# The first nine chunks of a recurrent layer, written as one list of 472 steps

## The chip, the core and the metric

The kernel runs on one core of a Trainium2 chip. Its engines are TensorE (PE, with its weight loads as PEld), VectorE (DVE), ScalarE (ACT), GpSimd (POOL) and SyncE (SP), which here issues nearly all DMAs. The metric is the device time of one execution in microseconds.

## What is computed

A recurrence over 768 time steps for 4 x 8 heads with a 40 x 40 state, and behind it two layers on the 3072 x 320 result, in float32:

```python
for t in range(S):
    y[:, :, t] = np.einsum('bhd,bhde->bhe', rt, state)
    Sa = np.einsum('bhde,bhe->bhd', state, at)
    state = state * wt[:, :, None, :] - np.einsum('bhd,bhe->bhde', Sa, bt)
    state = state + np.einsum('bhd,bhe->bhde', vt, kt)
...
h = np.maximum(np.maximum(x @ w1, x @ w2), x @ w3); x = h @ w_out              # Moe1, 768 wide
h = x @ w_in; g = h * np.tanh(softplus(h)); out = g @ w_out                    # Moe2, 2048 wide
```

## The kernel before

**Chunks, units, solves.** The recurrence is cut into chunks of 32 steps, two groups of 24, so 48 chunks. A *unit* is the preparation of two chunks (24 units, `pre`): a scan of the decays w on DVE (L253), logarithm and exponential on ScalarE for the inverse (L264, L266), two corrections on DVE (L276, L278), a square on ScalarE (L280), two scalings of the keys on DVE (L285, L287), four multiplications of ax on POOL (L272), 64 small matmuls into a PSUM bank, a copy to `ab` (ScalarE, L307), a transpose (DVE, L311) and four masks on POOL (L318). A *solve* takes the `ab` of four units: one transpose, then 31 pairs of a product and a subtraction, each on the result of the last (L346, L348), then a transpose back (L352). Solves 0 and 1 run on DVE, later ones on POOL. `kb` (L363, L367) transposes a unit's keys into `ls`.

**A chunk** (`chain`) has five stages, each on the result of the last: x0 (PE) and its copy X0 (ScalarE, L427); u; uT; the products on PE and rs on DVE (L461); ys on PE (L474), then the next state sv (L479) and YT (L481) on DVE. Chunk c needs its unit, the solve of the unit's four and sv of chunk c-1. Every second chunk's YT goes out by DMA to `xs`, from where Moe1 loads it.

**Weight tiles.** Moe1's weights come as 24 tiles of 64-bit numbers (18 of w1, w2, w3 and 6 of w_out). `from64` loads one into a staging buffer `raw`, of which there are four as of `t`; then one step on ScalarE and two on DVE (L672, L675, L676), one addition on POOL (L678), casts on ScalarE (L687) and two subtractions on POOL (L693, L732).

**Order.** `start` writes out units 0 to 3, solve 0 and the conversions beside it. `run` then goes through chunks and five slots of each: in a slot one stage of the chunk, `fill`, steps of the next units (`advance`), steps of the solve, and `kb`. Up to chunk 4 (`LAG`) `fill` takes one step of the pipelined conversions a slot; at chunk 4 it ends them and opens Moe1, whose groups of 256 tokens then take four chunks each: 18 products of seven matmuls, then 48 matmuls in steps of eight. Up to chunk 9 (`HAND`) all five engines issue in the order in which the program is written; behind it PE, DVE and ScalarE do, and the compiler orders POOL and SP. Each engine works strictly in its order, so what waits holds all that is queued behind it. Moe1's groups run on to the end of the chunks, then Moe2 follows.

Of the kernel before, what the change touches and what calls it, by code (L numbers as in the profile page):

```python
# [8 lines left out]
F32 = mybir.dt.float32  # L9
# [86 lines left out]
FREE = 0  # L96
CONV = 6
# [3 lines left out]
MID = 6  # L101
STEPS = (1, 1, 1, 1, 1)
HOLD = (7, 0)
CATCH = 8
# [59 lines left out]
class Attention:  # L164
# [56 lines left out]

    def load_w(self, n):
# [22 lines left out]
    def pre(self, n):  # L245
# [62 lines left out]
        if n < NB:  # L308
            yield
# [86 lines left out]
    def chain(self, c):  # L396
# [36 lines left out]
        yield  # L433
# [10 lines left out]
        yield  # L444
# [12 lines left out]
        yield  # L457
# [8 lines left out]
        yield  # L466
# [35 lines left out]
    def start(self, convert):  # L502
        nc, A = self.nc, self.A
        self.under, self.next, self.done, self.held, self.solved, self.turn = [], 0, 0, False, 0, 0
# [8 lines left out]
        nc.vector.memset(self.ax[0], 0.0)  # L513
        nc.vector.memset(self.zero, 0.0)
        nc.vector.memset(self.rst, 0.0)
        nc.vector.memset(self.rst[:, 0:528:C + 1], 1.0)
        for n in range(NB):
            if n:
                nc.gpsimd.memset(self.ax[n], 0.0)
            self.load_w(n)  # L520
            self.load_a(n)
            self.load_k(n)
        for t in self.sv:
            nc.gpsimd.memset(t, 0.0)
        nc.scalar.copy(out=self.ys.rearrange("p w x -> p (w x)")[:, 0:512], in_=self.rst[:, 0:512])
        nc.scalar.copy(out=self.ys.rearrange("p w x -> p (w x)")[:, 512:528], in_=self.rst[:, 512:528])
        for t in self.rs:
            zeros(t[32:64])
        for _ in range(3):
            convert()  # L530
        nc.sync.dma_start(out=self.cst, in_=A["cst"])
        for t in self.rs:
            nc.sync.dma_start(out=t[0:40, 4:9], in_=A["rsi"])
        self.load_v(0)
        self.load_chunk(0)
        nc.vector.memset(self.ls[0], 0.0)
        units = [self.pre(n) for n in range(NB)]
        self.next = NB

        def go(n, steps):  # L540
            for _ in range(steps):
                next(units[n], None)

        go(0, 2)
        nc.vector.memset(self.ls[1], 0.0)
        go(1, 2)
        go(0, 6)
        go(2, 2)
        go(1, 5)
        go(0, 2)  # L550
        go(1, 1)
        go(3, 2)
        go(2, 5)
        go(1, 2)
        go(2, 1)
        go(3, 5)
        go(2, 2)
        convert()
        go(3, 1)
        solve = self.solve(0)  # L560
        next(solve)
        go(3, 3)
        self.done = NB
# [822 lines left out]
```

## Time and profile before

| | |
|---|---|
| median of three runs | 1040.8 us (1040.03 to 1041.81) |
| the profiled execution | 1039.32 us, its span 1037.6 us |
| busy: PE, DVE, ACT, POOL | 914.8, 749.4, 735.7, 483.6 us |
| granted TensorE clock, mean | 0.958 of full speed |

The page's 40 slices of 25.9 us show PE at 4, 0, 3, 5, 6, 8, 7 tenths and then at 8 and 9; DVE begins at 8, 9, 7, 5, 6, 7, 8 tenths, POOL at 8, 4, 6, 8. The slices show that the first fifth of the time is another regime than the rest; they don't show which engine limits it, for which the stages have to be looked at one by one.

### The profile page before, as it was taken

The numbers are of one execution on the slowest core, as the hardware profiler recorded it, in microseconds if no ns is written. First come the engines' busy times: TensorE is split into PE (matmuls) and PEld (weight loads), VectorE is DVE, ScalarE is ACT, GpSimd is POOL, SyncE is SP. The second block draws the span as 40 slices with busy tenths as digits, with TensorE's granted clock in tenths as the row PEclk, the third lists the DMA queues.
The fourth block names the chain that finished last, engine by engine and source line by source line (L and its number), as shares of the span: only waits on it lengthen the run. The fifth ranks groups of instructions, "written<-read, shape, count | busy, mean of one in ns | idle before, by whom it ended". The sixth has DMA issues, their size and how long they took to land.

```text
span 1037.6 us, 34156 instructions
## 1 busy us (share of the span) xinstructions
PE 914.8 (88%) x14098; PEld 823.1 (79%) x14098; DVE 749.4 (72%) x1411; ACT 735.7 (71%) x1858; POOL 483.6 (47%) x715
## 2 busy tenths in 40 slices
PE   4035687899999999999999999979999999999996
PEld 3024576788889888898988988968898899889885
DVE  8975678566675556566366667698998888898875
ACT  5357644466777567577678977878797988878874
POOL 8468513569969947974943434780202011020000
PEclk9998586899999999999999999999999999999999
DMA  8638422345454444445356454420100010010000
GB/s 235 178 97 213 121 57 61 86 116 140 122 138 107 136 130 118 116 110 146 87 139 163 116 148 144 119 74 1 57 1 31 26 32 26 15 42 1 26 1 29
DMA packets 117334, 96.07 MB, mean 93 GB/s; under 512 B 73316, under 2 KB 93412, under 8 KB 117172
## 3 DMA queue, kind: packets, MB, share of 16 engines
q1 hardware_dynamic: 116432, 93.59, 33.4%
q8 instruction: 113, 1.85, 0.8%
q14 instruction: 49, 0.40, 0.1%
q10 hardware_dynamic: 740, 0.23, 0.1%
HBM read 81.20 MB, written 12.58 MB: 90 GB/s over the span
## 4 chain that ended last, share of the span: by engine, by line
PE 59%; DVE 14%; POOL 14%; ACT 6%; issue 5%; DMA 3%; SPq 0%; ACTq 0%; DVEq 0%; POOLq 0%
PE cops L1092 5%; PE cops L1093 5%; PE cops L1094 5%; PE ys L474 5%; PE cps L742 4%; PE cps L743 4%; PE cps L744 4%; PE bps L742 4%; PE bps L915 4%; POOL T L348 3%; POOL tv L346 3%; POOL ax L272 3%; PE bps L743 3%; PE bps L744 3%; PE cps L746 2%
## 5 line engine op out<-in xcount | busy, mean ns | idle before, releaser
L742 PE MATMUL bps<-bxh,bw 128*128 128x256 f32 x432 | 140.4, 326 | 4.6 <-DVE mx L874 3.4
L743 PE MATMUL bps<-bxl,bw 128*128 128x256 f32 x432 | 124.5, 288 | 3.3 <-DVE bxl L755 3.3
L744 PE MATMUL bps<-bxh,bw 128*128 128x256 f32 x432 | 123.2, 285 | 0.0
L1045 POOL CAST cxh<-cxl 128x512 fp32r<-128x512 f32 x15 | 12.0, 835 | 187.8 <-DMA cxl<-x 187.8
L742 PEld LDWEIGHTS bps<-bxh,bw 128*128 128x128 f32 x432 | 83.0, 192 | 13.7 <-DVE mx L874 3.8
L743 PEld LDWEIGHTS bps<-bxl,bw 128*128 128x128 f32 x432 | 83.8, 194 | 5.4 <-DVE bxl L755 5.4
L479 DVE TENSOR_TENSOR sv<-ys,pp 40x320 f32<-40x320 f32 x92 | 44.9, 488 | 55.6 <-PE ys L474 54.9
L744 PEld LDWEIGHTS bps<-bxh,bw 128*128 128x128 f32 x432 | 83.7, 194 | 0.0
L272 POOL TENSOR_TENSOR ax<-ax,pp 40x256 f32<-40x256 f32 x96 | 72.6, 774 | 20.9 <-DVE pp L253 9.3
L877 POOL TENSOR_TENSOR hl<-mx,hh 128x256 fp32r<-128x256 f32 x72 | 55.5, 771 | 56.0 <-ACT hh L876 54.8
L461 DVE TENSOR_TENSOR rs<-cgps,cst 64x256 f32<-64x256 f32 x96 | 40.6, 423 | 56.6 <-PE cgps L391 54.5
L1088 DVE TENSOR_TENSOR gl<-e,gh 128x512 fp32r<-128x512 f32 x93 | 69.9, 752 | 14.4 <-ACT gh L1087 13.4
L348 POOL TENSOR_TENSOR T<-T,tv 128x31 f32<-128x31 f32 (+15 forms) x124 | 74.7, 603 | 8.6
L318 POOL TENSOR_SCALAR_AFFINE_SELECT ax<-akT 32x256 f32<-32x256 f32 x96 | 49.0, 510 | 63.5 <-DVE akT L311 58.9
L915 PE MATMUL bps<-hh,bo 128*128 128x256 f32 x360 | 77.3, 297 | 0.6 <-ACT mx L872 0.6
L1076 ACT ACTIVATE e<-e 128x512 f32<-128x512 f32 x93 | 58.6, 630 | 24.9 <-DVE e L1074 24.4
L1080 DVE SCALAR_TENSOR_TENSOR e<-e,r 128x512 f32<-128x512 f32 x93 | 68.6, 737 | 8.7 <-ACT r L1078 8.6
L874 DVE TENSOR_TENSOR mx<-bps,mx 128x256 f32<-128x256 f32 x144 | 60.2, 418 | 19.4 <-ACT mx L872 11.7
L474 PE MATMUL ys<-rs,ls 128*40 128x72 f32 x1536 | 66.6, 247 | 7.9 <-DVE rs L461 5.7
L346 POOL TENSOR_TENSOR tv<-tr,T 128x31 f32<-128x31 f32 (+15 forms) x124 | 68.3, 551 | 11.2 <-DVE tr L339 3.0
L474 PEld LDWEIGHTS ys<-rs,ls 128*40 128x40 f32 x1536 | 57.8, 130 | 14.6 <-issue 5.8
L1073 ACT ACTIVATE e<-cps 128x512 f32<-128x512 f32 x93 | 54.7, 588 | 18.9 <-PE cps L746 18.8
(243 smaller groups left out, 3153.1 us busy)
## 6 DMA issues: line engine op xcount, KB each, us to landing
bk<-in_KB_dram SPq DMA_DIRECT2D x24, 448.0 KB
sv<-in_SV_dram SPq DMA_DIRECT2D x96, 80.0 KB
raw<-in_w_dram SPq DMA_DIRECT2D x18, 384.0 KB
again<-in_w_dram SPq DMA_DIRECT2D x27, 256.0 KB
w<-in_W_dram SPq DMA_DIRECT2D x21, 231.0 KB
v<-in_VT_dram SPq DMA_DIRECT2D x48, 96.0 KB
rs<-in_RT_dram SPq DMA_DIRECT2D x48, 96.0 KB
cxl<-x SPq DMA_DIRECT2D x12, 384.0 KB
```

The source lines that it names most:

```text
L272: nc.gpsimd.tensor_tensor(out=xv[:, h], in0=xv[:, h], in1=P[ro, h, 0:C], op=ALU.mult)
L346: eng.tensor_tensor(out=tv, in0=abT[:, s, s + 1:C].unsqueeze(2).to_broadcast([128, n, s + 1]), in1=T[:, s, 0:s + 1].unsqueeze(1).to_broadc ...
L348: eng.tensor_tensor(out=T[:, s + 1:C, 0:s + 1], in0=T[:, s + 1:C, 0:s + 1], in1=tv, op=ALU.subtract)
L474: nc.tensor.matmul(out=self.ys[64 * y:64 * y + 40, p, 0:72], lhsT=l[:, y, p], rhs=r_[:, :, 4 * (p % 4) + 2 * (1 - y) + p // 4], start=True ...
L742: nc.tensor.matmul(out=ps, lhsT=h[:, k], rhs=xh[:, k], start=(k == 0), stop=False)
L743: nc.tensor.matmul(out=ps, lhsT=h[:, k], rhs=xl[:, k], start=False, stop=False)
L744: nc.tensor.matmul(out=ps, lhsT=l[:, k], rhs=xh[:, k], start=False, stop=False)
L874: after(1, lambda ps=ps, mx=mx: nc.vector.tensor_tensor(out=mx, in0=ps, in1=mx, op=ALU.max))
L915: nc.tensor.matmul(out=pss[d][rows], lhsT=lhsT, rhs=rhs, start=first, stop=last)
L1076: nc.scalar.activation(out=e, in_=e, func=AF.Square, bias=1.0)
L1080: nc.vector.scalar_tensor_tensor(out=e, in0=e, scalar=1.0, in1=r, op0=ALU.add, op1=ALU.mult)
L1088: nc.vector.tensor_tensor(out=gl, in0=e, in1=gh.bitcast(F32), op=ALU.subtract)
```

## The change

`start` no longer ends with solve 0. It reads a list, `START`, of 472 entries, each a letter and a number, and does one step for each; the list goes to the end of chunk 8, and `run` begins at chunk 9. The letters: u a step of unit n, x its four multiplications of ax on POOL (now a step of their own, `mult`), c a stage of chunk n, e a step of solve n, w a step of weight tile n, f `fill` of a slot (chunk times five and slot), k half a `kb`; W, A, K, V, L the loads of a unit's w, a, keys, of a chunk's v and of a chunk; m, s, l, R, z, Z, U clears; p the constants of the scan, C, D loads of constants, r the first products.

Besides: a chunk's stage pauses once, not twice, and a slot takes one step of it; units 0 to 3 pause where later ones do; a tile pauses once behind its load, not three times; the two PSUM banks of Moe1 come from two pools of one in turn; each unit's bank for the inverse is named in `BANKS`, as it was before; `kb` of a unit waits until its keys are scaled.

The core of the diff (the removed body of `start`, which the words above tell, and the other four stages of the chunk, edited alike, are left out):

```diff
 NPOOL = 14
 NE = 3
-FREE = 0
-CONV = 6
 HAND = 9
 PACE = 2
 UD = 8
-MID = 6
-STEPS = (1, 1, 1, 1, 1)
+BEGIN = 9
+BANKS = 'ucucppxxssssssss'
+START = """
+m0 m1 K0 W0 W1 A0 W2 m2 A2 A1 K1 W3 K2 m3 A3 s1 V0 K3 w0 w1 w2 l1 s0 C l0 p R1 R0 u0 u0 u1 x0 u1 x1 u0 u0 u0
+u0 u2 u2 u0 u0 u0 u1 u1 x2 u0 u0 u1 u1 L0 u1 u1 u1 u3 x3 u3 u2 u2 u2 u2 u2 u2 u1 u1 u2 u3 u3 u3 l2 u3 u3 w3 u2
+w0 u2 u3 w0 u3 w1 w4 z5 A5 e0 L1 w1 u3 z6 A6 D w2 u3 e0 e0 e0 w5 z4 e0 e0 w1 e0 e0 w3 w0 r V1 e0 z7 A7 A4 e0
+w3 e0 w2 e0 e0 w0 e0 e0 w6 e0 e0 K4 K5 U w3 e0 e0 w1 e0 w4 e0 e0 e0 e0 w5 e0 e0 w6 w7 k0 w3 w5 w2 w2 k1 w5 w4
+w4 w4 w6 w8 w5 e0 e0 e0 e0 e0 e0 e0 e0 Z0 c0 w7 K6 w7 w6 c0 u4 w8 u4 c0 w9 w6 w10 w8 Z1 x4 w11 w12 w9 c0 w7 u4
+u4 w8 V2 c0 w11 w9 w13 u4 u5 w7 L2 w9 c1 A8 w8 w9 w10 w11 w10 k2 w14 w12 w10 u4 u5 x5 c1 w15 u5 w10 w11 u4 u4
+w12 w16 c1 w13 w11 w12 w14 c1 w13 w17 w14 u4 w18 u4 w15 w13 c1 u5 w12 k3 V3 w14 u5 K7 w13 w15 w19 w14 u4 w16
+u5 L3 w17 w17 u5 c2 w15 w16 w20 c2 u5 w18 c2 w15 w18 w19 u5 w17 w21 u5 c2 V4 c2 w18 k4 w17 u5 w19 w19 w20 c3
+w18 w22 w23 w20 L4 w20 K8 w21 c3 w23 w19 w20 c3 w21 w23 w22 k5 w21 c3 w22 w23 w23 A9 u6 w21 V5 w16 c3 w16 L5
+x6 w22 w22 c4 f20 u6 u6 c4 f21 u6 c4 u6 u6 u7 u7 c4 u7 V6 x7 f22 u6 u7 c4 K9 u7 u6 u6 u6 u6 L6 c5 f23 u7 u7 u7
+f24 f25 u7 e1 c5 f26 A10 u7 e1 e1 e1 e1 e1 c5 f27 c5 V7 f28 u7 e1 e1 e1 e1 c5 f29 k6 k7 e1 c6 c6 f30 c6 e1 e1
+L7 e1 e1 e1 f31 e1 e1 e1 c6 V8 e1 e1 e1 c6 k8 e1 f32 f33 e1 u8 u8 e1 L8 e1 e1 x8 c7 A11 e1 f34 u8 f35 e1 e1 u8
+c7 f36 u8 u8 e1 e1 c7 u8 u8 e1 u9 x9 u8 u9 f37 u8 e1 c7 u9 f38 u8 u9 c7 f39 V9 k9 L9 u9 K10 u9 u10 u10 u9 x10
+c8 f40 u10 u10 c8 f41 u9 u9 u9 c8 f42 u10 u11 x11 u9 c8 f43 K11 u10 c8 f44 u10 V10 u11 u11 L10
+"""
 HOLD = (7, 0)
+LAST = 8
...
+    def mult(self, n):
+
+        if n in self.multiplied:
+            return
+        self.multiplied.add(n)
+        x, P = self.ax[n % self.NX], self.pp[n % self.NP][0:R]
+        for y in range(2):
+            ro = slice(64 * y, 64 * y + 40)
+            xv = x[ro, y].rearrange("r p c t -> r (p c) t")
+
+            for h in (slice(0, 8), slice(8, 16)):
+                self.nc.gpsimd.tensor_tensor(out=xv[:, h], in0=xv[:, h], in1=P[ro, h, 0:C], op=ALU.mult)
...
         nc.scalar.activation(out=Q, in_=Q, func=AF.Exp, scale=-1.0, accum_out=self.gate.le(1e5, R))
-        for y in range(2):
-            ro = slice(64 * y, 64 * y + 40)
-            xv = x[ro, y].rearrange("r p c t -> r (p c) t")
-
-            for h in (slice(0, 8), slice(8, 16)):
-                nc.gpsimd.tensor_tensor(out=xv[:, h], in0=xv[:, h], in1=P[ro, h, 0:C], op=ALU.mult)
+        if not self.written:
+            self.mult(n)
         yield
 
         t = w.rearrange("r (q t) -> r q t", q=16)[0:R, :, 1:33]
...
         nc.vector.tensor_tensor(out=bv[:, 8:16], in0=bv[:, 8:16], in1=Qv[:, 8:16], op=ALU.mult)
-        if n >= NB:
-            yield
+        yield
+        self.scaled = n + 1
+        self.mult(n)
         while n >= NB and (self.turn < n or self.solved < self.batch[n]):
             yield
         if n < NB:
-            ps = self.ps_st.tile([128, 2, 4, 64], F32, name="m1", tag="b")
+            ps = self.ps_st[n % 2].tile([128, 2, 4, 64], F32, name="m1", tag="b")
         else:
             ps = self.ps_un.tile([128, 2, 4, 64], F32, name="m1", tag="un")
-        self.held = n >= NB
+            self.held = True
...
         nc.scalar.copy(out=self.ab[:, i:i + 8], in_=psv[:, :, C:2 * C])
-        if n < NB:
-            yield
+        yield
         akT = p1.tile([128, 4, 2, C], F32, name="akT")
...
         st_out(0)
         yield
-        yield
 
...
+        units, self.chains, self.solves = {}, {}, {}
+        steps = {}
+        def clean(n):
+            (nc.vector if n == 0 else nc.gpsimd).memset(self.ax[n], 0.0)
+        def unit(n):
+            if n not in units:
+                units[n] = self.pre(n)
+                steps[n] = 0
+            steps[n] += 1
+            if next(units[n], "end") == "end":
+                assert n == self.done, n
+                self.done += 1
+                del units[n]
+        def chain(c):
+            if c not in self.chains:
+                self.chains[c] = self.chain(c)
+            next(self.chains[c], None)
+        def substitute(k):
+            if k not in self.solves:
+                self.solves[k] = self.solve(k)
+            next(self.solves[k], None)
+        def constants():
+            nc.sync.dma_start(out=self.cst, in_=A["cst"])
+        def pattern():
+            nc.vector.memset(self.zero, 0.0)
+            nc.vector.memset(self.rst, 0.0)
+            nc.vector.memset(self.rst[:, 0:528:C + 1], 1.0)
+            nc.scalar.copy(out=self.ys.rearrange("p w x -> p (w x)")[:, 0:512], in_=self.rst[:, 0:512])
+            nc.scalar.copy(out=self.ys.rearrange("p w x -> p (w x)")[:, 512:528], in_=self.rst[:, 512:528])
+        def rows():
+            for t in self.rs:
+                nc.sync.dma_start(out=t[0:40, 4:9], in_=A["rsi"])
+        does = dict(u=unit, x=self.mult, c=chain, e=substitute, w=lambda t: next(tiles[t], None),
+                    f=lambda x: fill(x // 5, x % 5), p=lambda _: pattern(), C=lambda _: constants(), D=lambda _: rows(),
+                    Z=lambda i: zeros(self.ys[32:64, 4 * i:4 * i + 4]), z=lambda n: zeros(self.ax[n]), m=clean,
+                    s=lambda i: nc.gpsimd.memset(self.sv[i], 0.0), R=lambda i: zeros(self.rs[i][32:64]),
+                    l=lambda i: nc.vector.memset(self.ls[i], 0.0), U=lambda _: zeros(self.ud), W=self.load_w, A=self.load_a,
+                    K=self.load_k, V=self.load_v, L=self.load_chunk, k=lambda x: self.kb(x // 2, x % 2),
+                    r=lambda _: self.products(None, 0))
+        for x in START.split():
+            x, _, n = x.partition("*")
+            for _ in range(int(n or 1)):
+                does[x[0]](int(x[1:] or 0))
+        self.written = False
+        self.next = max(steps) + 1
+        self.under = [[units[n], steps[n]] for n in sorted(units)]
...
-        k, left = 0, 0
+        k = max(self.solves, default=-1)
+        solve = self.solves.get(k, iter(()))
+        left, due = (40, 2 * (self.last[k - 1] + 1)) if k in self.solves else (0, 0)
         halves = []
-        for c in range(NC):
+        for c in range(BEGIN, NC):
             n, cc = divmod(c, 2)
-            chain = self.chain(c)
+            chain = self.chains.get(c) or self.chain(c)
             if c == HAND:
...
-                if (c, slot) == (0, 4):
-                    for u in range(self.NK, AHEAD):
-                        self.load_k(u)
-                for _ in range(0 if c < FREE else PACE if LAG <= c < 2 * NB else 1):
-                    self.advance(min(NT, MID if c < LAG else AHEAD if (c, slot) < HOLD else 12 if c < CATCH else m + (cc == 1 and slot > 0)))
+                for _ in range(PACE if LAG <= c < LAST else 1):
+                    self.advance(min(NT, AHEAD if (c, slot) < HOLD else 12 if c < CATCH else m + (cc == 1 and slot > 0)))
...
-                next(chain, None)
                 if cc == 1 and slot in (0, 2) and n + 1 < NT:
                     halves.append((n + 1, slot // 2))
-                while halves and not self.held:
+                while halves and not self.held and halves[0][0] < self.scaled:
                     u, g = halves.pop(0)
...
-    for _ in range(3 if later else 2):
+    for _ in range(1 if later else 2):
...
-        self.ps = pool("b_ps", 2, space=PSUM)
+        self.ps = [pool(f"b_ps{i}", 1, space=PSUM) for i in range(2)]
-        self.banks = 2 * [self.ps]
+        self.banks = list(self.ps)
...
-                weights = pipelined(moe1.weights(), 1)
+                tiles = list(moe1.weights())
-                    for _ in range(STEPS[slot]):
-                        convert()
                     q, r = divmod(c - LAG, 4)
                     if q == 0 and (r, slot) == (0, 0):
-                        finish(weights)
+                        for t in tiles:
+                            finish(t)
                         moe1.open()
                     if (c, slot) == (2 * NB, 0):
                         moe1.third()
```

## Rows read from the trace of the kernel before

**Rows 1.** Windows: busy us by engine, instructions, clock, DMA share; cuts: chunk starts (L427).
```profile
core 0: us, PE busy (x) PEld busy (x) DVE busy (x) ACT busy (x) POOL busy (x), PEclk, DMA share, GB/s
0.00:24.70 24.70, 9.76 (x287) 8.31 (x288) 19.90 (x32) 13.77 (x31) 20.71 (x38) 1.00 0.90 233
24.70:58.30 33.60, 2.86 (x47) 2.00 (x43) 31.00 (x79) 11.50 (x26) 13.46 (x21) 1.00 0.59 159
...
60.80:74.50 13.70, 7.10 (x174) 5.72 (x174) 9.03 (x17) 9.56 (x29) 12.76 (x19) 1.00 0.39 120
74.50:92.30 17.80, 8.25 (x234) 6.69 (x235) 10.16 (x20) 12.52 (x38) 16.64 (x25) 1.00 0.83 224
92.30:105.90 13.60, 7.87 (x238) 6.38 (x240) 8.53 (x18) 8.67 (x27) 11.76 (x19) 0.58 0.66 181
105.90:116.60 10.70, 7.57 (x182) 6.33 (x184) 5.20 (x11) 7.79 (x23) 7.52 (x14) 0.50 0.33 86
116.60:129.10 12.50, 8.20 (x238) 6.86 (x239) 8.79 (x14) 7.82 (x24) 5.25 (x8) 0.50 0.59 135
129.10:147.40 18.30, 16.15 (x294) 14.25 (x294) 13.05 (x32) 6.72 (x20) 4.24 (x9) 0.73 0.21 51
147.40:164.80 17.40, 12.81 (x226) 11.40 (x226) 16.37 (x41) 5.14 (x17) 1.47 (x2) 0.80 0.24 54
164.80:189.70 24.90, 18.96 (x338) 16.46 (x334) 19.48 (x39) 13.50 (x37) 12.89 (x17) 0.73 0.27 75
189.70:205.80 16.10, 12.93 (x274) 11.59 (x274) 9.54 (x16) 6.71 (x22) 9.80 (x13) 0.79 0.33 86
205.80:638.00 432.20, 420.12 (x9434) 382.35 (x9431) 259.86 (x538) 311.17 (x972) 286.51 (x453) 0.99 0.48 125
```

**Rows 2.** Windows, as above: chunks 10 to 13, four of the later ones.
```profile
220.30:265.40 45.10, 43.83 (x1024) 39.92 (x1023) 28.06 (x54) 31.34 (x97) 39.49 (x64) 1.00 0.46 123
```

**Rows 3.** Windows, as above: stages A, B and C of the ramp.
```profile
0.00:60.80 60.80, 12.63 (x328) 10.31 (x328) 53.27 (x114) 27.61 (x60) 35.32 (x61) 1.00 0.69 183
60.80:116.60 55.80, 30.79 (x820) 25.12 (x822) 32.93 (x64) 38.55 (x114) 48.67 (x74) 0.80 0.59 161
116.60:205.80 89.20, 69.04 (x1354) 60.56 (x1353) 67.22 (x139) 39.89 (x116) 33.65 (x48) 0.72 0.31 76
```

**Rows 4.** POOL, 0 to 205.8: line op out<-in xcount | busy, mean ns | idle, releasers.
```profile
L272 POOL TENSOR_TENSOR ax<-ax,pp 40x256 f32<-40x256 f32 x48 | 33.8, 723 | 16.6 <-PE bps L746 7.0 <-DVE pp L253 5.9 <-PE kb L363 2.5
L678 POOL TENSOR_TENSOR t<-t,raw 128x384 int32<-128x384 int32 (+1 forms) x24 | 24.2, 1011 | 14.3 <-DVE t L676 13.1
...
L693 POOL TENSOR_TENSOR bw<-t,bw 128x256 fp32r<-128x256 f32 x18 | 13.1, 728 | 1.2 <-ACT bw L687 1.0
L732 POOL TENSOR_TENSOR bw<-t,bw 64x128 fp32r<-64x128 f32 x18 | 8.2, 454 | 1.4
```

**Rows 5.** The same view of ScalarE, 24.7 to 58.3.
```profile
L511 ACT COPY ax<-zero 128x1024 f32<-128x1024 f32 x4 | 3.9, 1038 | 0.0
```

**Rows 6.** Waits of DVE and of SP's queue, 0 to 206: total us, times, longest.
```profile
DVE t L676 <- POOL bw L732: 5.0, 4, 2.1
...
SPq L661 <- POOL t L678: 39.1, 13, 6.2
```

**Rows 7.** DVE by line, 0 to 205.8, columns as in rows 4.
```profile
L348 DVE TENSOR_TENSOR T<-T,tv 128x31 f32<-128x31 f32 (+15 forms) x62 | 21.0, 339 | 2.1
L676 DVE SCALAR_TENSOR_TENSOR t<-raw,bits 128x384 int32<-128x384 int32 (+1 forms) x24 | 12.9, 538 | 7.2 <-POOL bw L732 5.0
L675 DVE TENSOR_SCALAR bits<-raw 128x384 int32<-128x384 int32 (+1 forms) x24 | 12.9, 536 | 4.1 <-DMA raw<-in_wo_dram 2.5 <-DMA raw<-in_w_dram 1.4
L346 DVE TENSOR_TENSOR tv<-tr,T 128x31 f32<-128x31 f32 (+15 forms) x31 | 12.3, 396 | 0.8
```

**Rows 8.** Timeline of POOL and DVE at 143.7: start us, us, engine, line, operation.
```profile
143.75 0.73 POOL L877 TENSOR_TENSOR hl<-mx,hh 128x256 fp32r<-128x256 f32 x1 [4.92 <-ACT hh L876]
...
143.78 0.91 DVE L346 TENSOR_TENSOR tv<-tr,T 128x175 f32<-128x175 f32 x1
145.09 0.37 DVE L346 TENSOR_TENSOR tv<-tr,T 128x192 f32<-128x192 f32 x1
```

More of the change, by code (lines that the diff above doesn't have):

```diff
@@ L255, in pre @@
         yield
-        if NB <= n < 2 * NB:
-            Q = (self.ps_st if n < MID else self.extra).tile([128, 16, C], F32, name="Qx", tag="b")[0:R]
-        elif n >= NB:
+        where = BANKS[n] if n < len(BANKS) else "s"
+        if where == "s":
             Q = p1.tile([128, 16, C], F32, name="Q", tag="Q")[0:R]
-        elif n % 2:
+        elif where == "c":
             Q = self.cg[0:R].rearrange("p (q t) -> p q t", q=16)
+        elif where == "u":
+            Q = self.ps_un.tile([128, 16, C], F32, name="Qp", tag="un")[0:R]
         else:
-            Q = self.ps_un.tile([128, 16, C], F32, name="Qp", tag="un")[0:R]
+            Q = (self.ps_st[n % 2] if where == "p" else self.extra).tile([128, 16, C], F32, name="Qx", tag="b")[0:R]
         nc.scalar.activation(out=Q, in_=Pv, func=AF.Ln)
         nc.scalar.activation(out=Q, in_=Q, func=AF.Exp, scale=-1.0, accum_out=self.gate.le(1e5, R))
-        for y in range(2):
-            ro = slice(64 * y, 64 * y + 40)
-            xv = x[ro, y].rearrange("r p c t -> r (p c) t")
-            for h in (slice(0, 8), slice(8, 16)):
-                nc.gpsimd.tensor_tensor(out=xv[:, h], in0=xv[:, h], in1=P[ro, h, 0:C], op=ALU.mult)
+        if not self.written:
+            self.mult(n)
         yield
@@ L443, in chain @@
         st_out(1)
-        yield
         yield
@@ L500, in advance, with start @@
                 self.done += 1
-    def start(self, convert):
+    def start(self, tiles, fill):
         nc, A = self.nc, self.A
-        self.under, self.next, self.done, self.held, self.solved, self.turn = [], 0, 0, False, 0, 0
+        self.under, self.done, self.held, self.solved, self.turn = [], 0, False, 0, 0
+        self.written, self.multiplied, self.scaled = True, set(), 0
         def zeros(*ts):
@@ L511, in zeros @@
                 nc.scalar.copy(out=t, in_=z.to_broadcast(list(t.shape)))
[L513 to L529, printed above, removed]
-            convert()
[L531 to L563, printed above, removed]
-        self.turn = NB
-        convert()
-        nc.vector.memset(self.ls[2], 0.0)
-        zeros(self.ud)
-        self.products(None, 0)
-        self.load_v(1)
-        self.load_chunk(1)
-        for n in range(NB, AHEAD):
-            zeros(self.ax[n])
-            self.load_a(n)
-            if n < self.NK:
-                self.load_k(n)
-        for s in range(C - 1):
-            next(solve)
-            if s % CONV == CONV - 1:
-                convert()
@@ L580, in start @@
-        for g in range(2):
-            self.kb(0, g)
-        finish(solve)
-        for g in range(2):
-            zeros(self.ys[32:64, 4 * g:4 * g + 4])
+        units, self.chains, self.solves = {}, {}, {}
[11 more added lines that the diff above has]
+                del units[n]
@@ L586, in run @@
+        for x in START.split():
[5 more added lines that the diff above has]
+        self.under = [[units[n], steps[n]] for n in sorted(units)]
     def run(self, fill):
         NT, NC = 2 * NU, 2 * NCH
-        solve = iter(())
-        k, left = 0, 0
+        k = max(self.solves, default=-1)
+        solve = self.solves.get(k, iter(()))
+        left, due = (40, 2 * (self.last[k - 1] + 1)) if k in self.solves else (0, 0)
@@ L1332, in program @@
                 with tc.manual_schedule(engines=IN_ORDER | {mybir.EngineType.Activation, mybir.EngineType.Pool, mybir.EngineType.SP}):
-                    att.start(convert)
+                    att.start(tiles, fill)
                     next(chunks)
```

5 lines of the change are left out of this document (removed).

## The prediction

> **What bounds the kernel now.** I first read the busy time of each engine by stage, cut at the start of each chunk's first copy (X0, line 427). Behind chunk 9 the kernel is bound by TensorE: 420.1 of 432.2 us busy at a granted clock of 0.99, and four chunks with a whole Moe1 group take 45.1 us with 43.8 of them on PE [rows 1, 2]. So a chunk with its quarter of a group costs about 11 us there, and nothing of that part is edited. The list ends where chunk 9 begins, at 205.8 us. So the question is how early chunk 9 can begin; from there on each microsecond is kept, as long as the same work has been done by then.
>
> By then it has. The list issues fills 20 to 44, all 24 weight tiles, chunks 0 to 8, solves 0 and 1, transposes up to unit 4 and loads up to unit 11 and chunk 10; units 10 and 11 stand in the middle, as in the old trace. It is a permutation: DVE still has its 153.4 us, POOL its 117.7, ACT its 106.1 [rows 3]. The floor for chunk 9 is therefore about 158 us (DVE's sum and the 4.8 us that it is idle in the first 24.7, [rows 1]), and the most that can be won is 205.8 - 158 = 48 us.
>
> Then I asked stage by stage which engine is full. **A, 0 to 60.8**: DVE, 53.3 of 60.8 us [rows 3]. **B, chunks 0 to 3**: POOL, 48.7 of 55.8; DVE has only 32.9 [rows 3]. It converts weight tiles without a break, at 1.01 + 0.73 + 0.45 = 2.2 us for a tile [rows 4], and the chunks take 13.7, 17.8, 13.6 and 10.7 us where 11 would do [rows 1]. **C, chunks 4 to 8**: nobody for the whole stretch. DVE has 67.2 of 89.2 [rows 3]; it is nearly full in chunk 6 (16.4 of 17.4) and idle three to four tenths of the time in chunks 4, 5 and 8; the clock stands at 0.50 to 0.80 [rows 1].
>
> **The change, stage by stage.** *A.* The first solve keeps its place: the chain of 31 products and subtractions on DVE, 33.6 us with 31.0 busy, and five conversions go beside it in the list as in the trace [rows 1]. Ahead of it, unit 1's scan now runs while unit 0 waits for ScalarE, and the first two W loads come sooner; against it the load K0 is issued ahead of W0. DVE is busy 19.9 of the first 24.7 us [rows 1], so at most 4.8 us are there. I take -1, bounds -3 and +3. The clears of units 4 to 7 and the loads between the solve's steps are hidden: ACT is busy 11.5 of 33.6 us and the DMA engines 0.59 of it [rows 1]. Without that cover the four clears would cost 4 x 1.04 us [rows 5].
>
> *B.* The sum is made on POOL, since DVE's share is smaller. The list leaves some 17.6 of 24 tiles for this stage, and I count 49 us of POOL work from chunk 0's first step to chunk 4's, of which the last 2.7 (unit 6's four multiplications, 4 x 0.72 less overlap [rows 4]) need not be done when chunk 4 starts. So POOL alone allows 46 us. It is uneven: 8, 20, 7 and 14 us from chunk 0 on. What the chunks then take is the larger of that and their own 11: about 12, 16, 11 and 11, 50 us in place of 55.8. I take -6; bounds -10 (POOL's 46 exactly) and +2 (the waits of the next sentence). DVE's second conversion step waits for a staging buffer that POOL gives back, 5.0 us in four such waits [rows 6]; the same chunks' rs, sv and YT are queued on DVE behind it, and PE behind those. With two, three or four tiles in flight all through the list this wait stays; I leave it at its old size.
>
> *C.* The list puts the second solve's 34 steps between chunk 5's first step and chunk 7's fourth, in effect where they were, but with the other units between. Counting the list at the durations of the trace (a product 0.40 and a subtraction 0.34 in the mean [rows 7], the rest likewise), DVE gets 9, 15, 19, 17 and 7 us in chunks 4 to 8, 67 in all, as in the old trace [rows 3]. Where DVE has less than 11 the chunk's own chain decides, 11 to 12 us; where it has more, DVE does: 11.5 + 16 + 19 + 17 + 11.5 = 75 us in place of 89.2. I take -14. Bounds: -20 (chunk 8 and chunk 4 at 10.7, no gap on DVE) and 0 (the gaps of 5 to 7 us on DVE in chunks 5, 7 and 8 come back, at a low clock). PE is no second bound at full clock (11 us a chunk, [rows 2]); at half clock a chunk would want up to 22, and chunk 5 shows it: 16.2 of 18.3 us on PE at 0.73 [rows 1]. [...]
>
> One thing speaks against filling DVE and POOL side by side. While POOL ran a subtraction of 0.73 us, a product of the second solve took 0.91 us; the next, longer one took 0.37 [rows 8]. That is 0.5 us for a collision. The list puts two units' multiplications and two masks beside this solve, perhaps ten POOL instructions more than stood there; 0 to 5 us, and I take 1, within the 75. The Trainium skill, "SBUF — State Buffer", section "SBUF: two separate sides", says that a VectorE instruction with two SBUF inputs and a GpSimd one that reads SBUF exclude each other for the whole instruction; the row agrees in direction, and by the rule each collision would hold the loser for the rest of the other instruction, 0.7 us at most, some 5 to 7 us where I take 1.
>
> *Small edits, taken at nothing.* The multiplications of ax as a step of their own (x): the same four POOL instructions. One yield in a chunk's stage and one call in a slot: the same order behind chunk 9. Two one-bank pools in place of one of two banks, used in turn: the same rotation. One pause in place of three behind a tile's load matters only through the list. SP's queue gets W, A, K, V, chunk and weight loads in the list's order; in the old trace it waited 39.1 us in all for POOL to give staging back [rows 6], which cost only where a tile was then late. Bounds -2 and +4, in stage B.
>
> **Sum.** -1 - 6 - 14 = -21. Chunk 9 starts near 185 in place of 205.8 us. The profiled execution took 1039.3 us (1037.6 of span and 1.7 around it), 1.5 under the median of 1040.8; so 1018.3 against it and 1020 against the median.
>
> **The rivals.**
> *DVE filled almost whole.* If the interleaving leaves DVE hardly a gap, chunk 9 starts near 170: 36 us won, 1005. For it: DVE ran without a gap through chunk 6 already [rows 1]. Against it: DVE's work in chunks 2, 3, 4 and 8 is under 9 us each in the list, less than a chunk's chain.
> *Stage B moves, C doesn't.* If PE stays at half clock in chunks 5 to 7, they keep 18, 17 and 20 us or so, and C gives 5 at most: -1 - 3 - 3 = -7, 1034. For it: clock 0.73 to 0.80 in all three [rows 1]. Against: DVE, not PE, is the fuller engine in chunk 6.
> *The list does nothing to the end.* It would have to be that the Moe1 groups, not the chunks, set the time behind chunk 9 and are as late as before: 1040. Against it: the first group's fills are written at fixed places among the chunks.
> *Slower.* All five engines follow the written order through the ramp, and it is a new one, and four staging buffers are shared by 24 tiles. Tile 16's last two steps stand behind chunk 3's third stage, 50 and more entries after its third step; if a later tile's step on DVE or SP has to wait for that buffer, DVE stands still with the chunk behind it. Each such wait costs most of a chunk, some 10.7 us [rows 1]; one leaves a gain of 10, from the second on the change is lost, three give 1040.8 - 21 + 32 = 1052. Against it: the old waits of this kind were 2.1 us at most [rows 6].
>
> **How the numbers follow.** Forecast (gain 10 to 30) 0.63; DVE nearly full 0.12; B alone 0.13; nothing 0.04; slower 0.08. A measurement can tell about 0.2%, 2 us, from no change. The second rival's lower end falls within that by 0.01, and of "nothing" 0.01 falls past it, so faster is 0.63 + 0.12 + 0.12 = 0.87, same 0.04, slower 0.09. The range leaves out 2 in 10: it runs from 1005 (the first rival; the forecast's ends, -3 - 10 - 20, give 1007) to 1035 (just past the second rival), and leaves out the outer half of the first rival, a quarter of the second, and the last two.
>
> **What would show it.** Right in A: the first chunk's X0 copy at 57 to 62 us. In B: X0 of chunk 4 at 107 to 113, and POOL over 90% busy between. In C: chunks 5 to 7 at 15 to 19 us with DVE over 90% busy, chunks 4 and 8 under 13. X0 of chunk 9 at 180 to 190, and from it to the end 832 us as before. Wrong: DVE waits for POOL or a DMA of over 5 us in one piece, clock at 0.50 through chunk 6, or a stretch behind chunk 9 that is longer than 832 because POOL and SP, which are ordered anew there, fall otherwise.

## The result, and the profile after

The changed kernel takes 1033.06 us (median of five runs, 1030.22 to 1034.91), the kernel before beside it 1040.8 (1039.09 to 1042.47); the ratio of the two is on record as 0.9905, with a 95% interval of 0.9884 to 0.9926. So 8 us are won by the medians, 8 to 12 by the interval, where 21 were forecast. The direction and the range hold, the size doesn't.

The windows of the changed kernel, cut as [rows 1] at the start of each chunk's first copy (X0, now line 452), same columns; the first row is stage A, the next four B, the next five C, then chunk 9:

```profile
core 0: us, PE busy (x) PEld busy (x) DVE busy (x) ACT busy (x) POOL busy (x), PEclk, DMA share, GB/s
0.00:59.50 59.50, 12.62 (x328) 10.30 (x328) 52.57 (x113) 27.36 (x60) 37.90 (x64) 1.00 0.74 197
59.50:69.70 10.20, 5.58 (x165) 4.57 (x166) 6.74 (x13) 8.90 (x27) 9.29 (x15) 1.00 0.42 111
69.70:90.00 20.30, 11.47 (x276) 9.14 (x278) 16.16 (x31) 13.67 (x39) 18.89 (x28) 1.00 0.62 173
90.00:102.30 12.30, 8.53 (x214) 6.78 (x214) 5.07 (x12) 7.95 (x24) 8.51 (x14) 1.00 0.64 160
102.30:111.70 9.40, 5.90 (x168) 5.04 (x170) 6.34 (x12) 7.82 (x23) 8.08 (x12) 0.63 0.61 167
111.70:122.50 10.80, 8.17 (x240) 6.66 (x241) 7.73 (x13) 7.82 (x23) 7.48 (x13) 0.53 0.64 156
122.50:140.20 17.70, 15.34 (x298) 13.57 (x296) 14.75 (x36) 6.87 (x21) 5.13 (x9) 0.81 0.19 40
140.20:157.60 17.40, 11.40 (x214) 10.32 (x214) 16.27 (x41) 6.83 (x21) 2.17 (x3) 0.80 0.35 80
157.60:177.40 19.80, 16.41 (x332) 14.57 (x333) 17.30 (x36) 11.68 (x33) 11.33 (x18) 0.89 0.14 36
177.40:188.90 11.50, 11.31 (x277) 9.96 (x276) 9.07 (x15) 6.71 (x21) 7.68 (x11) 0.89 0.74 194
188.90:207.50 18.60, 15.46 (x328) 13.58 (x325) 10.72 (x21) 9.80 (x29) 6.23 (x10) 0.82 0.50 134
```

Against [rows 1, 3] the stages stand so (profiled executions: 1037.6 us of span before, 1033.2 after):

```
                       before    after    gain   forecast
A, to chunk 0            60.8     59.5    -1.3      -1
B, chunks 0 to 3         55.8     52.2    -3.6      -6
C, chunks 4 to 8         89.2     77.2   -12.0     -14
chunk 9 begins at       205.8    188.9   -16.9     -21
chunk 9 to the end      831.8    844.3   +12.5       0
```

The ramp (stages A to C) delivers 17 of the 21 us; 12.5 of them are lost again behind chunk 9, where the list has ended and where I had written that each microsecond is kept. By the medians the loss is smaller: the profile after is of the slowest of its five executions, the one before lies 1.5 us under its median, so that the net gain is 4.4 us by the profiles and 7.7 by the medians. Of the 12.5 us 9.7 are lost by the end of chunk 17, and there in few places. The length of single chunks, from X0 to X0:

```
chunk              9     14     17     21     25     29
before          14.6   11.2   11.4   11.1   11.4   11.1
after           18.6   14.9   13.0   11.8   12.2   11.8
```

Two waits name the two largest losses. The longest ones of PE and DVE in chunk 9 of the changed kernel (engine line waited for: us in all, times, longest):

```profile
DVE rs L483 <- PE cgps L416: 4.4, 1, 4.4
PE kb L388 <- ACT ls L392: 2.5, 1, 2.5
```

and in its chunk 14:

```profile
ACT mx L873 <- POOL hl L878: 4.8, 2, 3.9
DVE mx L875 <- ACT mx L873: 3.8, 1, 3.8
```

In chunk 9 of the kernel before there is no wait of kb for ls, and in its chunk 14 the wait of mx for hl is 2.1 us in two. (mx and hl belong to Moe1: ScalarE and then DVE gather its products in mx, and POOL forms hl from mx.) A kb is the transpose of half of a unit's keys; its two halves and the unit's own product m1 share one PSUM bank ("un"), so a unit that holds that bank longer makes both halves come late and close together.

### The profile page after: what moved, and what is told of

The parts are those of the page before. It is cut to its first block, busy times and chain, and to the rows that moved or that the text cites. A ratio compares the mean times of both kernels' runs of the same rounds, so it can differ in the third digit from the quotient of the medians.

```text
span 1033.2 us, 34141 instructions
## 1 busy us (share of the span) xinstructions
PE 917.4 (89%) x14098; PEld 824.6 (80%) x14098; DVE 752.2 (73%) x1411; ACT 735.3 (71%) x1858; POOL 479.4 (46%) x715
## 5 line engine op out<-in xcount | busy, mean ns | idle before, releaser
L1046 POOL CAST cxh<-cxl 128x512 fp32r<-128x512 f32 x15 | 13.1, 911 | 188.2 <-DMA cxl<-x 188.2
L248 POOL TENSOR_TENSOR ax<-ax,pp 40x256 f32<-40x256 f32 x96 | 69.2, 739 | 37.1 <-DVE pp L281 24.0
L1089 DVE TENSOR_TENSOR gl<-e,gh 128x512 fp32r<-128x512 f32 x93 | 69.9, 752 | 14.4 <-ACT gh L1088 13.4
L1077 ACT ACTIVATE e<-e 128x512 f32<-128x512 f32 x93 | 58.6, 630 | 25.4 <-DVE e L1075 25.0
L371 POOL TENSOR_TENSOR tv<-tr,T 128x31 f32<-128x31 f32 (+15 forms) x124 | 67.8, 547 | 11.1 <-DVE tr L364 2.6
L1074 ACT ACTIVATE e<-cps 128x512 f32<-128x512 f32 x93 | 54.7, 589 | 18.9 <-PE cps L747 18.8
```

Source lines behind the costliest of these rows:

```text
L248: self.nc.gpsimd.tensor_tensor(out=xv[:, h], in0=xv[:, h], in1=P[ro, h, 0:C], op=ALU.mult)
L371: eng.tensor_tensor(out=tv, in0=abT[:, s, s + 1:C].unsqueeze(2).to_broadcast([128, n, s + 1]), in1=T[:, s, 0:s + 1].unsqueeze(1).to_broadc ...
L1077: nc.scalar.activation(out=e, in_=e, func=AF.Square, bias=1.0)
L1089: nc.vector.tensor_tensor(out=gl, in0=e, in1=gh.bitcast(F32), op=ALU.subtract)
```

## The experiments

**Is the loss there each time?** The changed kernel once more, unaltered.

> The changed kernel once more, for a second trace. In the first one chunk 9 began 16.9 us earlier than before, but chunks 9, 14 and 17 then took 18.6, 14.9 and 13.0 us (14.6, 11.2 and 11.4 before). Theory 1 (an order written or compiled behind the list is worse): the same chunks are long again, within 1 us each. Theory 2 (an accident of that one execution): chunk 9 begins at 188 to 190 us again, but the long chunks are others or shorter, and the span is nearer to 1029.

1033.24 us, 0.9912 (0.9892 to 0.9932); chunk 9 takes 19.3, chunk 14 16.2, chunk 17 12.1. The loss belongs to the program. The length of chunk 9 is good to about 1 us between executions of the same ramp: 18.6, 19.3 and 18.3 in three executions with the changed kernel's order up to there, 14.6, 14.6 and 15.9 in three with that of the kernel before.

**Does unit 10 leave the list a step too early?** One step of unit 10 more at the list's end, and then two:

```diff
-c8 ... c8 f43 K11 u10 c8 f44 u10 V10 u11 u11 L10
+c8 ... c8 f43 K11 u10 c8 f44 u10 u10 V10 u11 u11 L10
```

> One entry more at the end of the list: unit 10's second half of matmuls (u10) ahead of V10. In the trace after the change, unit 10 frees its PSUM bank one slot later than before, so both halves of kb(5) come in one slot, the second waits 2.5 us for ScalarE's copies behind unit 12's logarithm, and chunk 9 takes 18.6 us instead of 14.6. Theory (the list ends one step short of the old state): chunk 9 takes 14 to 15 us and the median falls by 3 to 5 us against the changed kernel. Rival (PE's clock, at half from 197 to 204 us, and not the wait): chunk 9 stays above 17 us. If chunk 9 shrinks and the end does not move, a later wait takes the gain.

> The list with two more steps of unit 10 at its end (its second half of matmuls and the copy to ab), POOL ordered by the compiler. In that order 17 products and subtractions of solve 2 stand between chunk 12's second hl and the four multiplications ahead of chunk 14's first hl, and 19 ahead of that hl, as in the kernel before; with one more step of unit 10 they were 19 and 20, and chunk 14 took 13.4 us. Theory (the count of solve steps ahead of hl on a POOL that has no idle time is what chunk 14 loses by): chunk 9 at 15 to 16, chunk 14 at 11 to 12 us, the median 1 to 2.5 us under the list with one more step. Rival (POOL is late for another reason): chunk 14 stays at 13 or more.

One step: 1030.38 us, 0.9891 (0.9867 to 0.9915), chunk 9 15.7, chunk 14 13.4, chunk 17 12.1. Two: 1030.67 us, 0.9882 (0.9866 to 0.9898), chunk 9 16.6, chunk 14 12.0, chunk 17 12.1. So one unit that is a step behind makes the larger part of chunk 9's loss. But chunks 17, 21 and 25 keep their 12.1, 11.8 and 12.2: a step given to unit 10 doesn't reach units 12 and on. So I looked for something that every unit carries.

**Is it POOL's order?** POOL isn't among the engines that keep the written order behind the list; the compiler's planner orders it, and it falls otherwise in the two kernels. In chunk 13 begin 8 instructions of the third solve on POOL before, 11 after; one step of unit 10 leaves 11, two leave 9, with chunk 14 at 11.2, 14.9, 13.4 and 12.0. Here POOL is held to the written order behind chunk 9, in the changed kernel and in the one before:

```diff
-with tc.manual_schedule(engines=IN_ORDER | {mybir.EngineType.Activation}):
+with tc.manual_schedule(engines=IN_ORDER | {mybir.EngineType.Activation, mybir.EngineType.Pool}):
```

> The changed kernel with POOL kept in the written order behind chunk 9 too, in place of the compiler's. Theory (the compiler orders POOL anew from another starting point, and puts a unit's multiplications ahead of hl, on which Moe1's copies on ScalarE wait 3.9 us in chunk 14): chunks 14 and 17 at about 11 us, chunk 9 still near 18.6, 4 to 6 us less in all: ratio to the kernel before near 0.986. Rival (the written order is worse than the compiler's): solve 2's steps come later or earlier than they should and several chunks pass 12 us; slower than the changed kernel by 5 us or more.

> The kernel before with POOL kept in the written order behind chunk 9. It tells what that order costs or gives by itself. If it gives the kernel before as much as the changed one, POOL's order is no part of why the change gave less than forecast. Theory: the compiler's order suits the old ramp, so here 0 to 4 us slower than before. Rival: it gives 4 to 6 us here as well.

After: 1040.52 us, 0.9973 (0.9956 to 0.9991); before: 1042.57 us, 1.0004 (0.9991 to 1.0018). Chunk 14 takes 10.9 in both, but chunk 12 takes 20.7 and 19.5 instead of 11.6 and 11.9. The written order mends one chunk and breaks another; and chunk 9 stays at 18.3, so its loss isn't POOL's order. Then the written order only in chunks 13 to 15, or from chunk 13 on (both with the one step of unit 10), and from chunk 13 on in the kernel before; in these three the same line is split into blocks at chunk 13, in the first of them at chunk 16 too:

> The list with unit 10's step added, and POOL in the written order in chunks 13 to 15 alone. With the added step chunk 14 took 13.4 us and chunk 17 12.1, where hl stood behind solve steps and a unit's multiplications on POOL. Theory (that order of POOL is what chunk 14 loses by): chunk 14 at 10.9 to 11.5, the median 2 to 3 us under the list with unit 10's step. Rival (POOL is simply late by then): the loss moves to chunk 13, 15 or 16 and the median stays within 1 us.

> The same with POOL in the written order from chunk 13 to the end of the chunks. With that order from chunk 9 on, chunk 12 took 20 us in both kernels, the kernel before gained 3 us each in chunks 20 and 28, and the changed kernel did not. Theory (chunk 12 alone spoils that order): chunk 14 at 11, chunks 20 and 28 at 12 to 15, the median 3 to 8 us under the list with unit 10's step. Rival: chunks 20 and 28 grow to 16 as they did from chunk 9 on, no gain.

> The kernel before with POOL in the written order from chunk 13 on: the control of the run with the list. Theory (the kernel before loses nothing in chunk 14, so pinning gives it only what chunks 20 and 28 give): 3 to 7 us faster than before. If it gains as much as the list does by the same edit, the order of POOL is a matter of its own and not where the list's gain went.

1034.37 us, 0.9917 (0.9896 to 0.9938), chunk 14 18.1; 1035.71 us, 0.9944 (0.9923 to 0.9964), chunk 14 18.9; before 1041.49 us, 0.9997 (0.998 to 1.0013), chunk 14 16.4. My theory fell: I had taken the written order for the better one in chunk 14. But in the last run POOL makes chunk 14 long in the kernel before as well: 11 instead of 8 of the solve's instructions begin in chunk 13, and mx waits 5.4 us for hl in one piece. In all sixteen traces chunk 14 takes 10.9 to 12.0 us where 6 to 9 of them begin in chunk 13, and 13.4 to 18.9 where 11 do. With more of the solve ahead of a unit's multiplications, hl, for which ScalarE and then DVE wait, comes late. The count goes with the loss; no run changes the count alone.

**The extra pause.** One line is passed by all units behind the list. In the kernel before the `yield` behind the copy of `ab` is made by units 0 to 3 alone; the change drops the condition, so each later unit pauses there too. (The section on the change tells of the opposite case alone, units 0 to 3 pausing where later ones do; its diff shows this one.) The list has an entry for it; behind the list it is one slot in which the unit goes on holding the bank. The changed kernel with the pause only while the list is written, and the kernel before with the pause for units 10 and on:

```diff
 nc.scalar.copy(out=self.ab[:, i:i + 8], in_=psv[:, :, C:2 * C])
-yield
+if self.written:
+    yield
```
```diff
-if n < NB:
+if n < NB or n >= 10:
     yield
```

> The changed kernel with one edit: the pause behind the copy of a unit's bias rows (self.ab), which the change gives to every unit from 4 on, is made only while the list runs, so that the units behind the list go on as in the kernel before. All 472 entries of the list stay as they are. Theory (the extra pause, and not the list, gives back what the list won): X0 of chunk 9 begins near 189 as before this edit, chunk 9 takes about 14.6 instead of 18.6, chunk 14 about 11.2 instead of 14.9, chunk 17 11.4 instead of 13.0, chunks 21, 25, 29, 33 and 37 11.1 to 11.4 instead of 11.5 to 11.9; the solving of chunk 13 is again 8 instructions of POOL; about 1024 to 1027 us, ratio 0.983 to 0.987 against the kernel before. Rival (the loss behind chunk 9 is of the place in which the list hands over, and of POOL's order, whatever the units' pauses): chunks 9 and 14 stay over 16 and 13, about 1032.

> The kernel before with only the extra pause: units from 10 on pause once more behind the copy of their bias rows; ramp, order and everything else as before. Theory (the pause alone costs behind chunk 9): the ramp keeps its times (X0 of chunk 9 at 205.8), chunk 14 takes 13 to 15 instead of 11.2, chunks 17, 21, 25, 29, 33 and 37 each 0.3 to 0.8 more, chunk 9 perhaps more by up to 4; in all 4 to 10 us slower, ratio 1.004 to 1.010. Rival (the pause alone is harmless, the list's end is what matters): within 2 us of the kernel before, ratio 0.998 to 1.002, chunk 14 at 11 to 12.

Without the pause: **1023.24 us** (1021.46 to 1024.84), 0.9804 (0.9785 to 0.9824), span 1021.5. With it, the kernel before takes 1048.96 us, 1.0056 (1.0038 to 1.0074), span 1042.4. Chunk lengths:

```
chunk                    9     14     17     21     25     29   from chunk 9 to the end
before                 14.6   11.2   11.4   11.1   11.4   11.1   831.8
before with the pause  18.3   11.9   12.2   11.8   12.2   11.8   836.0
after                  18.6   14.9   13.0   11.8   12.2   11.8   844.3
after without it       16.2   11.2   11.4   11.2   11.4   10.6   833.2
```

The pause, the only edit in that run, makes chunk 9 of the kernel before 3.7 us longer, to the length of the changed kernel, and chunks 17, 21, 25 and 29 longer by 0.7 or 0.8, the last three again to its lengths. The wait of kb comes with it. Chunk 9 of the kernel before with the pause:

```profile
DVE rs L461 <- PE cgps L391: 4.4, 1, 4.4
PE kb L363 <- ACT ls L367: 2.4, 1, 2.4
```

Chunk 9 of the changed kernel without it has neither. The two halves of kb on PE there, and then in the changed kernel (start us, us, what; in brackets the idle time before and what ended it):

```profile
191.97 0.52 PE L389 MATMUL kb<-cst,bk 104*128 104x104 f32 x4
193.50 0.52 PE L389 MATMUL kb<-cst,bk 104*128 104x104 f32 x4
```
```profile
194.56 0.57 PE L388 MATMUL kb<-cst,bk 104*128 104x104 f32 x4 [0.64 <-DVE akT L336]
197.63 0.95 PE L388 MATMUL kb<-cst,bk 104*128 104x104 f32 x4 [2.50 <-ACT ls L392]
```

Counted from the chunk's start (188.3 and 188.9) the first half is there at 3.7 us without the pause and at 5.7 with it, the second at 5.2 and 8.7. With the pause the first half waits for akT, whose copy gives the bank back, and the second for ScalarE to read the first out of the bank; its four transposes run at half clock and take 0.95 us for 0.52:

```profile
197.50:198.60 1.10, 0.97 (x10) 0.72 (x14) 0.00 (x0) 0.08 (x1) 1.00 (x3) 0.50 0.00 0
```

Without the pause POOL's order, too, falls as in the kernel before. POOL by line in chunk 13 (with the instructions that cross its borders), the two lines of the solve, after and then after without the pause:

```profile
L373 POOL TENSOR_TENSOR T<-T,tv 128x256 f32<-128x256 f32 (+5 forms) x6 | 5.6, 931 | 0.4
L371 POOL TENSOR_TENSOR tv<-tr,T 128x256 f32<-128x256 f32 (+5 forms) x6 | 4.2, 699 | 0.5
```
```profile
L372 POOL TENSOR_TENSOR tv<-tr,T 128x255 f32<-128x255 f32 (+3 forms) x4 | 3.9, 969 | 0.3
L374 POOL TENSOR_TENSOR T<-T,tv 128x256 f32<-128x256 f32 (+4 forms) x5 | 3.8, 761 | 0.4
```

In chunk 14 the wait of mx is then as in the kernel before:

```profile
ACT mx L874 <- POOL hl L879: 2.2, 2, 1.8
```

So of the 12.5 us the pause accounts for 11.1 by these profiles (844.3 - 833.2), and by the medians for 10. What remains, 1.4 us, is about what chunk 9 still takes more (16.2 for 14.6). In the kernel before the pause costs less, 4.2 us by the profiles (836.0 - 831.8) and 5.8 by the medians, the profiled execution being the fastest of its six. There only 9 of the solve's instructions begin in chunk 13 and chunk 14 takes 11.9, and chunks 20 and 28 become shorter (13.1 and 12.5 us for 15.3 and 14.7). That the planner puts 11 there in the one and 9 in the other I have seen, not explained.

**What the rest of the list is worth.** The list is cut behind chunk 3 (its first 311 entries), and the old loop takes over from chunk 4; a condition in `run` is fitted to that, for no solve is under way there. The first cut leaves out the load of unit 9's keys; the second has it; the third has it and no pause behind the list:

```diff
-BEGIN = 9
+BEGIN = 4
```

> The list cut ahead of chunk 4 (its first 311 entries); chunks 4 to 8 are issued by the loop of the kernel before, slot by slot. Stages A and B gave 4.8 us in the trace after the change, stage C 12.1. Theory (the list's order of chunks 4 to 8 gives C's part by itself): chunk 4 begins at 111 to 113, chunk 9 at 199 to 202, and as that loop leaves unit 10 where the kernel before left it, chunk 9 takes 14 to 16 us. Rival (C became shorter because A and B ended earlier and with denser PE work): chunk 9 begins at 189 to 193 although the list says nothing of these chunks.

> The list cut ahead of chunk 4 once more, now with the load of unit 9's keys (K9), which the cut had left out, at its end; chunks 4 to 8 by the loop of the kernel before. In the run without that load chunk 9 began at 200.6 us, 5.2 us earlier than in the kernel before, and the end came 5 us later. Theory (C's gain is the list's own, and chunks 9, 14, 20 and 28 take back more than A and B gave, for POOL's compiled order has the longer run of solve steps): chunk 9 near 200, chunk 14 at 14.5 to 16, the end 0 to 6 us later than the kernel before. Rival (the missing load had disturbed it): the end 3 to 6 us earlier than the kernel before, the 5 us kept.

> The changed kernel with the list cut behind chunk 3 (first 311 steps, with the load of unit 9's keys) and without the extra pause behind the list: chunks 4 on are ordered by the old loop, as in the kernel before. Theory (chunks 4 to 8 are shortened by the list's order there): X0 of chunk 4 near 112, chunks 4 to 8 take 85 to 90 as in the kernel before (89.2), X0 of chunk 9 at 198 to 203, behind it about 832; 1034 to 1039 us, ratio 0.992 to 0.998. Rival (the old loop was held up in chunks 4 to 8 only by what came late out of the ramp, so the shorter ramp helps there by itself): X0 of chunk 9 at 188 to 192, about 1025, ratio 0.984.

1046.78 us, 1.0039 (1.0024 to 1.0054); 1047.18, 1.0035 (1.0019 to 1.0051); 1045.5, 1.0024 (1.0007 to 1.0042). Windows of the third, chunks 4 to 8:

```profile
112.20:130.00 17.80, 9.28 (x270) 7.57 (x269) 11.43 (x18) 7.87 (x23) 9.15 (x16) 0.92 0.51 118
130.00:147.30 17.30, 15.56 (x264) 13.93 (x265) 10.44 (x26) 6.88 (x21) 2.49 (x5) 0.69 0.15 44
147.30:165.60 18.30, 12.85 (x226) 11.52 (x224) 17.18 (x43) 5.12 (x17) 1.47 (x2) 0.81 0.25 54
165.60:190.30 24.70, 19.54 (x338) 17.28 (x334) 18.77 (x36) 13.48 (x37) 12.89 (x17) 0.72 0.29 77
190.30:206.90 16.60, 14.01 (x274) 12.67 (x274) 9.54 (x16) 6.75 (x22) 9.74 (x13) 0.69 0.30 81
```

Chunk 9 begins at 206.9, later than the 198 to 203 of the theory and far from the rival's 188 to 192. Chunks 5 to 8 take 76.9 us, as in the kernel before (76.7, [rows 1]): the earlier start of chunk 4 alone shortens none of them. But in the two cuts that keep the pause the same chunks, by the same old loop, take 70.1 and 68.8 (chunk 9 at 200.6 and 199.2), and 66.4 in the changed kernel. So with the old loop's order the pause alone takes 7 to 8 us off these chunks, of the 10.3 that the list takes off. (Among the eight traces with the whole list and x5 in it they vary from 65.2 to 69.1 us, among the four with the order of the kernel before from 76.1 to 78.3.) Some 5 us of it lie in chunk 8, which takes 16.1 us in the kernel before and 16.6 in the third cut. In both, DVE stands in front of akT until ScalarE has copied `ab`, 5.0 us in the one and 4.6 in the other; with the pause akT stands a slot later, and chunk 8 of the second cut has no such wait. The wait in the third cut, and chunk 8 of the second:

```profile
DVE akT L336 <- ACT ab L332: 4.6, 1, 4.6
```
```profile
187.60:199.20 11.60, 11.24 (x274) 10.12 (x274) 9.36 (x15) 6.71 (x23) 9.81 (x15) 0.85 0.36 92
```

The same pause thus wins time in stage C and loses it behind chunk 9 (845.6 and 845.8 us with it, 839.4 without). The list holds it as one entry of each unit; how much of C's 12 us is this entry and how much the rest of the order no run separates. Chunk 4 takes 17.8 where it took 12.5; the hand-over eats what A and B had won. A place of hand-over has a price of its own: this kernel, without the pause behind the list, still needs 839.4 us behind chunk 9, with 17.4 in chunk 9 and 16.2 in chunk 12. In that chunk 18 of the solve's instructions begin on POOL; the two kernels with POOL in the written order from chunk 9 on have 24 and 18 there, and all others 13 or 14 and 11.2 to 11.9 us. Why the planner puts them there I have not followed.

**Is chunk 1 POOL's?** POOL is busy 18.9 of its 20.3 us. In the kernel without the pause the entry x5 is left out, which moves unit 5's four multiplications behind its seventh step; nothing is left out of the computation.

```diff
-... w14 w12 w10 u4 u5 x5 c1 w15 u5 ...
+... w14 w12 w10 u4 u5 c1 w15 u5 ...
```

> As the run without the extra pause behind the list, but the entry x5 is left out of the list, so that unit 5's four multiplications on POOL stand behind its seventh step, in chunk 2, and no longer in chunk 1. Nothing is left out of the computation. Theory (chunk 1 is POOL's, which is busy 18.9 of its 20.3 us, and chunk 2 is not, 8.9 of 11.7): chunk 1 takes 17 to 18.3, chunk 2 11.7 to 13, X0 of chunk 3 is 1 to 3 us earlier, about 1021 to 1023 us. Rival (DVE's waits for staging or the chunk's own chain set chunk 1): chunk 1 stays at 19.5 to 20.5, X0 of chunk 3 does not come earlier or comes later as unit 5 is later, 1023 to 1026.

1029.63 us, 0.988 (0.9862 to 0.9899): chunk 1 takes 25.4, worse than either theory had it. The waits of chunk 1 in this run:

```profile
PE m L328 <- POOL ax L248: 9.4, 2, 9.2
ACT X L453 <- PE x0ps L450: 9.0, 2, 7.9
```

The multiplications (ax) are late, PE stands in front of unit 5's product m for 9.2 us, and chunk 2's X0 is queued behind it on PE. So in this run POOL sets the end of chunk 1, by way of a product that stands ahead of the chunk on PE: pushed back, the multiplications only keep that product waiting, and all that is queued behind it. Whether POOL sets the end of chunk 1 with x5 in its place the run doesn't show, for it fits neither theory: there PE's longest waits in chunk 1, in the same product, are 3.8 us in two for DVE's scaled keys and 3.1 for POOL.

## Why the prediction was partly right

**The step that failed** is the one under "Small edits, taken at nothing", with the two statements at the start that go with it: of the part behind chunk 9 "nothing of that part is edited", and "from there on each microsecond is kept". I listed pools, yields in the chunk's stage and the pauses of a tile's load, and did not cost the pause that each unit from 4 on gets. It is one slot per unit, in the steady part that no line of the list touches, and it costs 11.1 us there by the profiles, 10 by the medians. With that line put right the kernel takes 1023.24 us, 20 under the median of the kernel before on the same chip; the forecast was 21. That these agree so closely is partly luck: by the profiles it is 16.1 us (1037.6 - 1021.5), made of 17.5 by chunk 9 and 1.4 lost behind it. I should have asked of each edit to a routine whether units behind the list pass through it, and which bank, queue or order they hold meanwhile. The sign that I had named ("a stretch behind chunk 9 that is longer than 832 because POOL and SP, which are ordered anew there, fall otherwise") came up, but the order was a consequence; the pause was the cause, and the bank a second way for its cost. The entry was wrong in the other direction too: under the old loop the pause shortens chunks 5 to 8 by 7 to 8 us.

**Stage A**: -1 forecast, -1.3 measured.

**Stage B**: -6 forecast, -3.6. POOL's shares were counted as 8, 20, 7 and 14 us and came to 9.3, 18.9, 8.5 and 8.1, so the last one was wrong. The sum didn't follow its own rule either: the larger of each share and 11 is 11 + 20 + 11 + 14 = 56, no gain at all, and I evened it out to 12, 16, 11 and 11. The chunks took 10.2, 20.3, 12.3 and 9.4. Chunk 1 has POOL's share whole, and in the run without x5 nothing of it could slide into chunk 2; 11 is no floor in this stage. POOL was busy 44.8 of 52.2 us, 86%, less than the 90% that was to show the mechanism. The wait of DVE's second conversion step for staging [rows 6], which I left at 5.0 us, is gone from DVE's waits in this stretch. The rival that made the kernel slower by waits for staging didn't happen.

**Stage C**: -14 forecast, -12.0: 10.8, 17.7, 17.4, 19.8 and 11.5 for the 11.5, 16, 19, 17 and 11.5 of the sum. DVE is 65.1 of 77.2 us busy, less than the 67.2 of [rows 3], and in chunks 5 to 7 it is 83, 94 and 87% busy, where over 90% was to show that DVE decides; in chunk 5 PE had more, 15.3 of 17.7 us at a clock of 0.81. And the cuts behind chunk 3 show that some of the gain comes with the pause, which the sum doesn't have. The price that I put on DVE and POOL working side by side (1 us) did not show: the 31 products of the second solve took 0.383 us in the mean, 0.396 before, and its subtractions 0.339 and 0.340. But the ten more POOL instructions beside that solve were miscounted: 12 ran there where 9 had. Products of over 0.6 us were three before (0.91, 0.74, 0.72) and two after (0.90, 0.83); each of the five ended 0.1 to 0.3 us behind the POOL instruction that it ran beside. The 5 to 7 us by the rule of the Trainium skill ("SBUF — State Buffer", section "SBUF: two separate sides") were therefore not put to a test; the five products agree with that rule. The rival that C doesn't move because of the clock fell: at 0.80 to 0.89 chunks 5 to 7 came to 54.9 us from 60.6.

**The rivals' ending**: the time landed on the 1034 that I had given the rival "B moves, C doesn't", by another cause.

## What to carry to other kernels

An edit that lets a hand-written stretch say more (a pause, a step of its own) is also passed by all the work that isn't written by hand; cost it there, at the number of units that pass it, before calling it nothing. When a change to a ramp wins less than the ramp shows, cut the trace where the change ends and compare the chunks behind it one by one: a loss that comes back every four chunks, here 0.7 or 0.8 us in 21, 25 and 29, had its cause in what every unit carries, not in the ramp. And of uneven work on one engine each stage takes its own largest share; a mean over the stages is a bound and not an estimate.

## What was not expected of the hardware

The clock column of the early rows can't be taken at its word. Chunk 4 of the changed kernel stands at 0.53 above, and without the pause, by the same part of the list, at 1.00:

```profile
112.20:123.10 10.90, 8.36 (x240) 6.81 (x241) 7.90 (x13) 7.82 (x24) 7.40 (x12) 1.00 0.63 165
```

The pause isn't the reason: the second execution of the changed kernel shows 1.00 there too. And the matmuls that can be compared are equally long. The 128x128 transposes of u (utps) in chunk 4 of the changed kernel, in chunk 4 without the pause, and in chunk 10 of the changed kernel, where the row's clock is 1.00:

```profile
L472 PE MATMUL utps<-cst,ud 128*128 128x128 f32 x2 | 0.7, 448 | 1.4 <-ACT ud L464 1.4
L473 PE MATMUL utps<-cst,ud 128*128 128x128 f32 x2 | 0.7, 448 | 1.4 <-ACT ud L465 1.4
L472 PE MATMUL utps<-cst,ud 128*128 128x128 f32 x2 | 0.4, 272 | 0.0
```

The first change of the clock that the trace without the pause holds is at 123.0 us; in the changed kernel it is at 101.4, in the kernel before at 91.1. In all sixteen traces each utps ahead of the first change took 417 to 477 ns; behind it they took 415 to 477 where the clock stood at 0.50 and 270 to 332 where it stood at 1.00. So the 1.00 of the rows ahead of that time, in [rows 1] those of stage A and of chunks 0 and 1, says only that the trace holds no change yet; by the durations of utps PE ran at the lower level (1.2 of 2.4 GHz) from chunk 0 to that time. What these chunks would take at the upper level no run shows.
